# Transformer block of 2048 tokens: attention output of blocks 2 to 14 turned by transposing transfers, values of eight heads in one stretch, another count for row tilings

## The chip, the cores and the metric

The program runs on one core of a Trainium2 chip. The metric is the time of one execution in microseconds of the device, median of several runs; lower is better. TensorE (PE) does the matrix products, VectorE (DVE) and ScalarE (ACT) the work element by element, GpSimd (POOL) the selects of the mask, SyncE (SP) issues most transfers. Each engine takes its instructions in the order in which they were written into the program.

## The reference

One transformer block, all in float32: S = 2048 tokens of D = 640, 32 heads of 20 with a causal window of 256 keys, and a gated feed-forward part of 1536.

```python
def _layernorm(x, axis=-1, eps=1e-5):
    m = jnp.mean(x, axis=axis, keepdims=True)
    v = jnp.var(x, axis=axis, keepdims=True)
    return (x - m) / jnp.sqrt(v + eps)

def _A_ref(x, wqkv, wo):
    ...
    q, k, v = qkv[0], qkv[1], qkv[2]
    scores = jnp.einsum("bhqd,bhkd->bhqk", q, k) * (Dh ** -0.5)
    idx = jnp.arange(S)
    mask = (idx[:, None] - idx[None, :] >= 0) & (idx[:, None] - idx[None, :] < W)
    scores = jnp.where(mask[None, None], scores, -1e9)
    p = _softmax(scores, axis=-1)
    o = jnp.einsum("bhqk,bhkd->bhqd", p, v)
    return (lambda x, *d: x.transpose(*d))(o, 0, 2, 1, 3).reshape(B, S, D) @ wo

def _B_ref(x, w_gate, w_up, w_down):
    return (_gelu(x @ w_gate) * (x @ w_up)) @ w_down

x = A_x
h = x + _A_ref(_layernorm(x, axis=-1), A_wqkv, A_wo)
h2 = h + _B_ref(_layernorm(h, axis=-1), B_w_gate, B_w_up, B_w_down)
```

## The kernel before

**Staging.** The tokens are cut into 16 blocks of 128. For each block x is loaded and normalised, split into a high and a low float16 part (`xh`, `xl`) and turned, so that the features lie on the partitions. Q and K are made for two blocks at a time, V for one. Every dense product is the sum of three float16 products (high by high, high by low, low by high), which stand in the profile as matmuls on `mm` with weights such as `w0h` and `w0l`. The feed-forward part comes last, after the attention of all blocks; its first pieces begin while the last blocks' attention runs.

**Attention of a block.** For each pair of heads the scores are made twice. First with queries on the partitions (`maxima`, line 833): 60 rows of the array, two heads side by side on its two halves, into `ra` or `rb`, a tile of two PSUM banks each. VectorE adds the band of the mask and reduces each head's 320 scores to the row's maximum `mxs` in one instruction (`max_out`, line 905), which writes the masked scores as bf16 into `junk`. Then with keys on the partitions (`scores`, line 950), with two more rows that carry the maxima, again into `ra` or `rb`. ScalarE takes the exponential into `pt` (`score_out`, line 988), and GpSimd sets to zero what lies outside the window: three `affine_select` for four heads at once where a block has three key blocks. `pt` is a ring of three tiles, each with four heads. The values (`value_lane`, line 1015) are float32 products of 128 rows by 21 columns, four heads on the four column groups of the array, 24 records for four heads, into `pv`. After 16 heads `pv` is copied to `oT`, four transposes and a division bring it back to rows as `o32` (`normalise`, line 1041).

**The attention output.** `o_transpose` (line 1062) turns the 128x640 of `o32` on TensorE with the identity: four chunks of 128 into `tp`, then the fifth. ScalarE casts `tp` to `oh`, VectorE subtracts to `ol`. Both are the weights that stay in the array for the output projection (`wo_block`, line 1080). There is one buffer of `tp`.

**x by transfers.** Blocks of x from the fifth on (`x_lane`, line 673) are turned another way, by `turned` (line 505): ScalarE casts x to float16 in the first half of a buffer `xp`, VectorE writes the rest into the second half, and SyncE issues two transposing transfers, `xh<-xp` and `xl<-xp`. `xp` has one buffer, and a counter (`opened["xparts"]`) lets only one block into it at a time, until the second transfer has been issued.

**What sets the order.** Nothing is scheduled by hand. The builder keeps a clock for each engine (`Clock`, line 54) and gives every instruction a modelled duration (`Engine.cost`, line 214). Each piece of work is a generator that yields the engine it needs and the time at which its data are there by that model. The loop at the end of `block_kernel` picks, again and again, the first of its lanes that can start: results that come out of PSUM, transposes, the row lane (`maxima` and `scores`), the value lane, and the dense lane. So a changed duration, or a changed wait, moves instructions on all engines. For TensorE the model adds 0.095 us where the form changes between full, row (64 rows or less) and column (32 columns or less), and counts a matmul beside the previous one, on another part of the array, almost at nothing:

```python
switch, k.mode = SWITCH * (k.mode != mode), mode
...
beside, k.half = mode != "full" and at > k.half and not switch, at
if beside:
    return 0.004
return switch + k.warmth(max(n * passes / 2400, 0.027), rows) + 0.0027
```

All instructions carry line 199, where the wrapper calls the real engine; the names of the tiles tell them apart.

Of the kernel before, what the change touches and what calls it, by code (L numbers as in the profile page):

```python
# [11 lines left out]
F32 = mybir.dt.float32  # L12
F16 = mybir.dt.float16
BF16 = mybir.dt.bfloat16
# [8 lines left out]
P = 128  # L23
# [166 lines left out]
class Engine:  # L190
# [23 lines left out]
    def cost(self, op, out, ins):  # L214
# [39 lines left out]
def block_kernel(ctx: ExitStack, tc: tile.TileContext, x, wqkv, wo, wg, wu, wd, out):  # L254
# [87 lines left out]
    ones = const.tile([P, P], F32, name="ones")  # L342
    nc.vector.memset(ones, 1.0)
# [251 lines left out]
    mask = wp.tile([P, 2 * P], F32, name="mask")  # L595
# [3 lines left out]
    band = wp.tile([P, 5 * HB], F32, name="band")  # L599
# [11 lines left out]
    RV, RK = 5, 6  # L611
# [101 lines left out]
    def load_x(j):  # L713
        if 0 < j < NR:
            t = at("pt", [P, 4, 3, P], F32, 3).rearrange("p a b c -> p (a b c)")
# [98 lines left out]
    def pairs(j):  # L814

        return 2 if j < 2 else 1
# [42 lines left out]
    def row_need():  # L859
# [45 lines left out]
    def max_out(j, pr, par, ps, at_):  # L905
        b = B[j]
        n = len(window(j))
        for k in range(pairs(j)):
# [3 lines left out]
            junk = at("junk", [P, 5 * HB], BF16, 1)  # L912
            nc.vector.tensor_tensor_reduce(junk[:, :w], head,
# [36 lines left out]
    def scores(at_):  # L950
        j, pr = scoreq.popleft()
        b = B[j]
        u = pr // 2
        if pr % 2 == 0:
            b.pt[u] = at("pt", [P, 4, 3, P], F32, 3)
            pos["units"] += 1
# [21 lines left out]
        tasks.append(score_out(j, pr, t, b.pt[u], at_))  # L978
# [9 lines left out]
    def score_out(j, pr, t, pt, at_):  # L988
        b = B[j]
        u = pr // 2  # L990
        n = len(window(j))
        m = pairs(j)
        yield on("scalar", t)
        w = min(n * P, 5 * HB)
        for k in range(m):
            h = 2 * (pr % 2 + k)
            nc.scalar.activation(pt[:, h:h + 2].rearrange("p h a b -> p h (a b)")[:, :, :w],
                                 t[:, :, k * n * P:k * n * P + w], AF.Exp, scale=esc)
# [5 lines left out]
        if n == 3:  # L1004
            half = pt.rearrange("p h a (b c) -> p h (a b) c", b=2)
            for a, (i, o) in enumerate(((0, 0), (3, 5))):
                nc.gpsimd.affine_select(half[:, :, o], half[:, :, i], pattern=[[0, 4], [-1, HB]],
                                        compare_op=ALU.is_ge, fill=0.0, base=-1 - HB * a,
                                        channel_multiplier=1)
        diag = part(pt, n, n - 1).rearrange("p h a b -> p h (a b)")  # L1010
        nc.gpsimd.affine_select(diag, diag, pattern=[[0, 4], [1, P]],
                                compare_op=ALU.is_ge, fill=0.0, base=0, channel_multiplier=-1)
        valq.append((j, u))

    def value_lane():

        while True:
            yield pe(when=lambda: valq and B[valq[0][0]].v == 2 and pos["ones"])
            j, u = valq.popleft()
            b = B[j]  # L1020
            pt = b.pt.pop(u)
# [3 lines left out]
            yield pe(pt, pv[:, u % 4, :])  # L1025
            for k, i in enumerate(order):
                for c in range(4):
                    nc.tensor.matmul(pv[32 * c:32 * c + DH + 1, u % 4, :].rearrange(
                                         "p (a b) -> p a b", b=HB),
                                     vring[ks[i] % RV][:, 4 * u + c, :], part(pt, n, i)[:, c],  # L1030
                                     start=(k == 0), stop=(k == n - 1))
            pos["values"] += 1
# [664 lines left out]
```

## Time and profile before

| | |
|---|---|
| median of three runs | 1022.17 us (1020.41 to 1023.81) |
| the profiled execution | 1023.17 us |
| its span, from first to last instruction | 1021.3 us |
| granted TensorE clock, mean | 1.000 |
| transposes of the attention output on TensorE, `tp<-ident,o` | 80 records, 15.0 us busy, 286 ns each |
| row maxima of 320 scores on VectorE | 448, 219.1 us busy, 489 ns each |
| selects of the mask on GpSimd, `pt<-pt` | 352, 175.3 us busy, 513 ns each |
| values, `pv<-pt,v`, four heads | 24 records, 0.85 us |

The page's first part gives the busy time of each engine and its share of the span, with the number of instructions. A busy TensorE is not the same as TensorE at its peak, since matmuls overlap and their ends are modelled. The groups give, for one kind of instruction by the names of its tiles, its count, its busy time, the mean of one in ns, and the idle time of the engine just before it with what ended it. In a timeline a row is: start in us, duration, engine, line, operation, what it writes and reads, shapes, and in brackets the idle time ahead of it and its releaser. For TensorE the shape 60*64 means 60 rows by 64 columns of the array.

### The profile page before, as it was taken

To read this page: it belongs to the slowest core of one execution; us is meant where nothing else is said; L and a number is where in the kernel's file an instruction comes from. 1 tells how busy PE (TensorE), PEld (TensorE's weight loads), DVE (VectorE), ACT (ScalarE), POOL (GpSimd) and SP (SyncE) were. 2 spreads that over 40 slices of the span, in tenths; PEclk is the share of its full clock that TensorE was granted. 3 is DMA by queue.
4 is the path that set the end of the run, shared out by engine and by line. 5 is a ranking of instruction groups with operands and counts; after the bars stand their busy time and mean duration, and the time that the engine had idled before them with its cause. 6 is when DMAs were issued, how large, how long until landed. Compare 5 with 4: busy or idle time off the path is not lost.

```text
span 1021.3 us, 30777 instructions
## 1 busy us (share of the span) xinstructions
PE 999.8 (98%) x12921; PEld 695.8 (68%) x12921; DVE 754.8 (74%) x2221; ACT 437.0 (43%) x706; POOL 298.0 (29%) x489
## 2 busy tenths in 40 slices
PE   8999999999999999999999999999999999999998
PEld 7875666676666676776655564567777777777776
DVE  6888998986787787474788788798996975544553
ACT  6514654656555564654558543522222222221220
POOL 7102223443343342342436321255313310000000
PEclk9999999999999999999999999999999999999999
DMA  8657667361551524225033433223553532222211
GB/s 306 137 116 175 184 145 168 81 163 55 91 122 44 114 57 118 42 61 127 3 131 106 92 117 103 78 104 127 161 177 90 161 138 78 78 96 86 78 53 52
DMA packets 105835, 112.67 MB, mean 110 GB/s; under 512 B 38369, under 2 KB 79585, under 8 KB 105697
## 3 DMA queue, kind: packets, MB, share of 16 engines
q1 hardware_dynamic: 93600, 99.97, 35.9%
q10 hardware_dynamic: 12096, 10.75, 3.4%
q8 instruction: 101, 1.65, 0.7%
q14 instruction: 38, 0.30, 0.1%
HBM read 73.73 MB, written 28.84 MB: 100 GB/s over the span
## 4 chain that ended last, share of the span: by engine, by line
PE 82%; DVE 8%; DMA 4%; ACT 2%; issue 2%; SPq 1%; POOL 0%; ACTq 0%; DVEq 0%
PE mm L199 41%; PE pv L199 12%; PE ra L199 11%; PE rb L199 10%; PE tp L199 7%; DVE junk L199 2%; DVE am L199 1%; DVE ht L199 1%; DMA v<-in_wqkv_dram 1%; DMA gu<-in_wqkv_dram 1%; SPq L199 1%; DMA qT<-mT 1%; DVE m L199 1%; ACT pt L199 1%; DMA h_dram<-ht 1%
## 5 line engine op out<-in xcount | busy, mean ns | idle before, releaser
L199 POOL TENSOR_SCALAR_AFFINE_SELECT pt<-pt 128x512 f32<-128x512 f32 x352 | 175.3, 513 | 278.2 <-ACT pt L199 262.6
L199 DVE CUSTOM_DVE_ANT_0 junk<-rb,band 128x320 bf16<-128x320 f32 x230 | 112.5, 489 | 41.3 <-PE rb L199 35.9
L199 DVE CUSTOM_DVE_ANT_0 junk<-ra,band 128x320 bf16<-128x320 f32 x218 | 106.6, 489 | 43.8 <-PE ra L199 38.3
L199 ACT ACTIVATE pt<-ra,esc 128x640 f32<-128x640 f32 (+2 forms) x131 | 99.6, 767 | 66.2 <-PE ra L199 53.3
L199 ACT ACTIVATE pt<-rb,esc 128x640 f32<-128x640 f32 (+2 forms) x125 | 94.9, 766 | 77.2 <-PE rb L199 56.5
L199 PE MATMUL pv<-pt,v 128*21 128x128 f32 x2880 | 104.1, 275 | 1.1 <-ACT oT L199 1.1
L199 PEld LDWEIGHTS <-ah 128*128 128x128 f16 x768 | 75.0, 98 | 29.5 <-issue 2.1
L199 ACT ACTIVATE gel<-gel,ffk 128x512 f32<-128x512 f32 x36 | 26.0, 721 | 138.0 <-DVE gel L199 138.0
L199 PEld LDWEIGHTS pv<-pt,v 128*21 128x21 f32 x2880 | 68.6, 100 | 11.9 <-issue 2.1
L199 PEld LDWEIGHTS <-ws 128*128 128x128 f16 x720 | 70.3, 98 | 8.3
L199 PEld LDWEIGHTS <-kT 62*64 62x64 f16 x2880 | 61.9, 107 | 13.9 <-issue 10.1
L199 PEld LDWEIGHTS <-qT 60*64 60x64 f16 x1280 | 29.8, 104 | 60.3 <-issue 51.3
L199 PEld LDWEIGHTS <-gu 128*128 128x128 f16 x440 | 42.1, 98 | 36.1 <-issue 2.5
L199 DVE SCALAR_TENSOR_TENSOR ht<-mm,ffk,ht 128x320 f32<-128x320 f32 x96 | 52.1, 545 | 10.9 <-PE mm L199 9.0
L199 ACT CAST ah<-gel 128x512 f16<-128x512 f32 x48 | 29.6, 617 | 64.4 <-DVE gel L199 64.2
L199 PE MATMUL mm<-xh,w1h 128*128 128x256 f16 x200 | 54.7, 274 | 1.3 <-DVE qks L199 1.3
L199 PE MATMUL mm<-xl,w1h 128*128 128x256 f16 x200 | 54.7, 273 | 0.0
L199 PE MATMUL mm<-xh,w1l 128*128 128x256 f16 x200 | 54.7, 273 | 0.0
L199 PE MATMUL mm<-w3l,oh 128*128 128x320 f16 x160 | 48.1, 301 | 0.1
L199 PE MATMUL mm<-w2h,xh 128*128 128x320 f16 x160 | 48.1, 300 | 0.0
L199 PE MATMUL mm<-w2h,xl 128*128 128x320 f16 x160 | 48.1, 301 | 0.0
L199 PE MATMUL mm<-w3h,ol 128*128 128x320 f16 x160 | 48.1, 300 | 0.0
(299 smaller groups left out, 2521.3 us busy)
## 6 DMA issues: line engine op xcount, KB each, us to landing
ws<-wsums SPq DMA_DIRECT2D x24, 640.0 KB
qk<-qks ACTq DMA_DIRECT2D x32, 256.0 KB
qT<-qk SPq DMA_DIRECT2D x48, 160.0 KB
kT<-qk SPq DMA_DIRECT2D x48, 160.0 KB
wsums<-ws SPq DMA_DIRECT2D x12, 640.0 KB
ht<-in_x_dram SPq DMA_DIRECT2D x16, 320.0 KB
h_dram<-ht SPq DMA_DIRECT2D x16, 320.0 KB
ht<-h_dram SPq DMA_DIRECT2D x16, 320.0 KB
```

Of the source, the lines that this page charges most:

```text
L199: r = real(*args, **kw)
```

## The change

- *Count of row tilings.* In the builder's clock a matmul beside the last one, on another part of the array, counts 0.0005 us in place of 0.004.
- *Row maxima.* `tensor_tensor_reduce` writes its masked scores back to the PSUM that it reads; `junk` is gone. `mask` and `band` become bf16. The constant `ones` is dropped.
- *Exponentials.* The ring `pt` has seven tiles of two heads in place of three of four. GpSimd's selects go over two heads at a time, so there are twice as many of half the size. A part of the ring is free again when the values of its group of four are made.
- *Values.* The value lane waits for two groups of four heads and writes both in one stretch, 48 records instead of 24.
- *Attention output.* For blocks 2 to 14 `o_transpose` goes through `turned`, as x does: a cast on ScalarE into `xp`, a subtraction on VectorE, and two transposing transfers into `oh` and `ol` on SyncE. It shares `xp` and its counter with x. Blocks 0, 1 and 15 stay on TensorE.

```diff
@@ Engine.cost
             if beside:
-                return 0.004
+                return 0.0005
...
-    mask = wp.tile([P, 2 * P], F32, name="mask")
+    mask = wp.tile([P, 2 * P], BF16, name="mask")
...
-    band = wp.tile([P, 5 * HB], F32, name="band")
+    band = wp.tile([P, 5 * HB], BF16, name="band")
...
-    RV, RK = 5, 6
+    RV, RK, RP = 5, 6, 7
...
@@ row_need
-        free = 3 - (pos["units"] - pos["values"])
+        free = RP - (pos["parts"] - 2 * pos["values"])
         for j, pr in list(scoreq)[:2]:
             b = B[j]
-            free -= pr % 2 == 0
+            free -= pairs(j)
...
@@ max_out
-            junk = at("junk", [P, 5 * HB], BF16, 1)
-            nc.vector.tensor_tensor_reduce(junk[:, :w], head,
+            nc.vector.tensor_tensor_reduce(head, head,
                                            band if n == 3 else mask[:, (2 - n) * P:], 1.0,
                                            -3.0e38, ALU.add, ALU.max,
...
@@ scores
-        if pr % 2 == 0:
-            b.pt[u] = at("pt", [P, 4, 3, P], F32, 3)
-            pos["units"] += 1
+        for k in range(pairs(j)):
+            b.pt[pr + k] = at("pt", [P, 2, 3, P], F32, RP)
+        pos["parts"] += pairs(j)
...
@@ score_out
-        pos[j, u] += 2 * m
-        if pos[j, u] < 4:
-            return
-        yield on("gpsimd", pt[:, :, 0, :])
...
+        for k in range(pr, pr + pairs(j)):
+            pt = b.pt[k]
+            yield on("gpsimd", pt[:, :, 0, :])
+            if n == 3:
...
+            diag = part(pt, n, n - 1).rearrange("p h a b -> p h (a b)")
+            nc.gpsimd.affine_select(diag, diag, pattern=[[0, 2], [1, P]],
+                                    compare_op=ALU.is_ge, fill=0.0, base=0, channel_multiplier=-1)
+            pos[j, "u", k // 2] += 1
+            if pos[j, "u", k // 2] == 2:
+                valq.append((j, k // 2))
...
@@ value_lane
-            yield pe(when=lambda: valq and B[valq[0][0]].v == 2 and pos["ones"])
-            j, u = valq.popleft()
+            yield pe(when=lambda: len(valq) > 1 and B[valq[0][0]].v == 2 and pos["ones"])
+            j, u = valq[1]
...
-            yield pe(pt, pv[:, u % 4, :])
...
+            yield pe(*(b.pt[k] for k in range(2 * u - 2, 2 * u + 2)),
+                     pv[:, u % 4 - 1:u % 4 + 1, :])
+            for u in (u - 1, u):
...
@@ o_transpose
+        if 2 <= j < 15:
+            def dst():
+                b.oh, b.ol = at("oh", [P, KC, P], F16), at("ol", [P, KC, P], F16)
+                return b.oh, b.ol
+
+            yield on("scalar", src, when=lambda: not opened["xparts"] and B[j - 2].wrote)
+            yield from turned(src, None, None, dst, None, at("xp", [P, D], F32, 1))
+            b.normal = True
+            woq.append(j)
+            return
```

`turned`, which the change calls and does not touch:

```python
key = "xparts" if dst else "parts"
yield on("scalar", src, when=lambda: not opened[key] and (not when or when()))
opened[key] += 1
two = (two if dst else lnbuf[2]).bitcast(F16)
hi, lo = two[:, :D], two[:, D:]
nc.scalar.copy(hi, src)
yield on("vector", hi)
nc.vector.tensor_tensor(lo, src, hi, op=ALU.subtract)
if dst:
    to = dst()
for o, i in zip(to, (hi, lo)):
    yield ("sync",), need(i, eng="sync")
    nc.sync.dma_start_transpose(o, i)
opened[key] -= 1
```

Where the instructions stand. On TensorE, before, in the middle of the attention: one group's values (`pv`, of the exponentials `pt`) between a row tiling (`rb`) and the transposes of the attention output (`tp<-ident,o32`).

```order
L199 LDWEIGHTS kT_124
L199 MATMUL rb_7857<-qT_5631,kT_124 64x64
L199 MATMUL pv_125<-pt_7729,v3_122 21x128 x4
L199 MATMUL pv_125<-pt_7729,v2_121 21x128 x4
L199 MATMUL pv_125<-pt_7729,v4_123 21x128 x4
L199 MATMUL tp_7890<-ident_78,o32_7496 128x128 x4
L199 LDWEIGHTS w0h_144
L199 MATMUL mm_7753<-xl_5821,w0h_144 128x256
```

On TensorE of the changed kernel, the same kind of place (of the second group, `pt_6855` and `pt_6895`, the first key block is shown):

```order
L199 MATMUL mm_6945<-w2h_158,xl_2530 128x320
L199 MATMUL pv_123<-pt_6770,v1_118 21x128 x2
L199 MATMUL pv_123<-pt_6824,v1_118 21x128 x2
L199 MATMUL pv_123<-pt_6770,v0_117 21x128 x2
L199 MATMUL pv_123<-pt_6824,v0_117 21x128 x2
L199 MATMUL pv_123<-pt_6770,v2_119 21x128 x2
L199 MATMUL pv_123<-pt_6824,v2_119 21x128 x2
L199 MATMUL pv_123<-pt_6855,v1_118 21x128 x2
L199 MATMUL pv_123<-pt_6895,v1_118 21x128 x2
```

The values of two groups now follow one another, each group from two tiles of `pt`, and no transposes of `o32` come behind.

On VectorE, before, within one block's row maxima (`mxs`; the reads of the accumulator between the reductions are left out):

```order
L199 ISA junk_7066,mxs_5633<-ra_7046,band_105 128x320
L199 ISA junk_7108,mxs_5633<-rb_7078,band_105 128x320
L199 SCALAR_TENSOR_TENSOR ht_5735<-mm_7038,hsc_128,ht_5735 128x320
L199 ISA junk_7155,mxs_5633<-ra_7128,band_105 128x320
L199 RECIPROCAL rec_7154<-tp_7149 128x16
L199 TENSOR_TENSOR o32_6806<-tp_7149,rec_7154 128x320
L199 ISA junk_7191,mxs_5633<-rb_7170,band_105 128x320
```

On VectorE of the changed kernel, again within one block's maxima:

```order
L199 ISA ra_7300,mxs_5534<-ra_7300,band_103 128x320
L199 BN_STATS lstx_7352<-xt_5989 128x6
L199 SCALAR_TENSOR_TENSOR ht_6383<-mm_7251,hsc_126,ht_6383 128x320
L199 BN_AGGR lmvx_7382<-lstx_7352 128x2
L199 ISA ra_7359,mxs_5534<-ra_7359,band_103 128x320
L199 RECIPROCAL rec_7395<-tp_7390 128x16
L199 TENSOR_TENSOR o32_7389<-tp_7390,rec_7395 128x320
L199 ISA ra_7400,mxs_5534<-ra_7400,band_103 128x320
```

Each reduction stands there twice, once for each head of the pair, and is shown once. Before, the maxima take `ra` and `rb` in turn; now they go into `ra` three times, one fill after the other, with the scores in `rb`.

On SyncE of the changed kernel, with the transfers of the attention output between a store of the residual stream (`h_dram`) and loads of x and of the queries:

```order
L199 DMA h_dram_72<-ht_4756 128x640
L199 DMA ht_6383<-in_x_dram 128x640
L199 DMA_TRANSPOSE oh_6414<-xp_6376 128x5x128
L199 DMA_TRANSPOSE ol_6415<-xp_6376 128x5x128
L199 DMA h_dram_72<-ht_5403 128x640
L199 DMA qT_6998<-qk50_5637 20x16x256 x3
```

The two transposing transfers are new in this queue; before, the loads and stores follow one another there.

More of the change, by code (lines that the diff above doesn't have):

```diff
@@ L341, in block_kernel @@
     nc.vector.memset(mhalf, -0.5)
-    ones = const.tile([P, P], F32, name="ones")
-    nc.vector.memset(ones, 1.0)
     NS = 16
@@ L986, in part, with score_out @@
         return (half[:, :, 0:6:5], half[:, :, 1:3], half[:, :, 3:5])[i]
-    def score_out(j, pr, t, pt, at_):
+    def score_out(j, pr, t, at_):
         b = B[j]
-        u = pr // 2
         n = len(window(j))
-        m = pairs(j)
+        w = min(n * P, 5 * HB)
         yield on("scalar", t)
[L994 to L997, printed above, removed]
+        for k in range(pairs(j)):
+            nc.scalar.activation(b.pt[pr + k].rearrange("p h a b -> p h (a b)")[:, :, :w],
@@ L1024, in value_lane @@
             order = [1, 0, 2] if n == 3 else list(range(n))
-            yield pe(pt, pv[:, u % 4, :])
[L1026 to L1032, printed above, removed]
+            yield pe(*(b.pt[k] for k in range(2 * u - 2, 2 * u + 2)),
+                     pv[:, u % 4 - 1:u % 4 + 1, :])
+            for u in (u - 1, u):
+                valq.popleft()
+                pt = [b.pt.pop(k) for k in (2 * u, 2 * u + 1)]
+                for k, i in enumerate(order):
+                    for c in range(4):
+                        nc.tensor.matmul(pv[32 * c:32 * c + DH + 1, u % 4, :].rearrange(
+                                             "p (a b) -> p a b", b=HB),
+                                         vring[ks[i] % RV][:, 4 * u + c, :],
+                                         part(pt[c // 2], n, i)[:, c % 2],
+                                         start=(k == 0), stop=(k == n - 1))
+                pos["values"] += 1
             if u % 4 == 3:
```

21 lines of the change are left out of this document (7 added, 14 removed).

## Prediction

> **What bounds the kernel now.** I read the page's busy times first, then its chain of waits, then the table of stretches of 50 us.
>
> ```profile
> span 1021.3 us, 30777 instructions
> ...
> PE 999.8 (98%) x12921; PEld 695.8 (68%) x12921; DVE 754.8 (74%) x2221; ACT 437.0 (43%) x706; POOL 298.0 (29%) x489
> ...
> PE 82%; DVE 8%; DMA 4%; ACT 2%; issue 2%; SPq 1%; POOL 0%; ACTq 0%; DVEq 0%
> ...
> core 0: us, PE busy (x) PEld busy (x) DVE busy (x) ACT busy (x) POOL busy (x), PEclk, DMA share, GB/s
> ...
> 100.00:150.00 50.00, 48.47 (x801) 33.26 (x794) 46.69 (x158) 29.71 (x52) 14.22 (x26) 1.00 0.64 155
> 150.00:200.00 50.00, 47.68 (x796) 33.20 (x794) 44.60 (x160) 28.73 (x48) 17.14 (x34) 1.00 0.54 142
> ...
> 400.00:450.00 50.00, 49.78 (x1012) 34.62 (x1010) 30.00 (x112) 25.07 (x40) 17.05 (x37) 1.00 0.23 61
> ```
>
> TensorE works without a real break and its clock is granted in full: time goes only where PE gets less to do, and comes back where PE has to wait. VectorE is the neighbour to watch: from 100 to 200 us it is busy 91.3 of 100 us, while at 400 to 450 us it has 20 us of 50 free. The profiled execution took 1023.17 us, 1.9 more than its span and 1.0 more than the median of 1022.17; I sum against 1023.2 and take off 1.0 at the end.
>
> **Term 1: changes of tiling.** TensorE's own line of time shows what leaving one form of matmul for another costs (start in us, duration, what is written and read, rows*columns of the array, shapes).
>
> ```profile
> 301.86 0.27 PE L199 MATMUL mm<-xh,w0l 128*128 128x256 f16 x1
> 302.06 0.33 PE L199 MATMUL rb<-kT,qT 60*64 60x320 f16 x4
> 302.22 0.31 PE L199 MATMUL ra<-qT,kT 62*64 62x128 f16 x12
> 302.46 0.85 PE L199 MATMUL pv<-pt,v 128*21 128x128 f32 x24
> ...
> 303.37 0.27 PE L199 MATMUL mm<-xl,w1h 128*128 128x256 f16 x1
> 303.48 0.27 PE L199 MATMUL mm<-xh,w1l 128*128 128x256 f16 x1
> ```
>
> Equal dense matmuls of 256 columns start 0.11 us apart (303.37 to 303.48). Where a row tiling (60*64, 62*64) follows the same dense matmul, the step is 0.20 (301.86 to 302.06). A change of form thus costs 0.09; from one row group to another (302.06 to 302.22) there is none. Counted over the whole order, dense, row and column (128*21) matmuls change places 657 times before and 569 times after: stretches of the 24 value records fall from 128 to 64, of 48 records each. 88 changes by 0.09 are **7.9 us** less PE work.
>
> **Term 2: transposes of the attention output.** The same line of time where the five chunks of one block's output are turned, four together and the fifth later:
>
> ```profile
> 306.59 0.66 PE L199 MATMUL tp<-ident,o 128*128 128x128 f32 x4
> 307.18 0.33 PE L199 MATMUL ra<-kT,qT 60*64 60x320 f16 x4
> ...
> 309.96 0.33 PE L199 MATMUL tp<-ident,o 128*128 128x128 f32 x1
> 310.13 0.27 PE L199 MATMUL mm<-xh,w1l 128*128 128x256 f16 x1
> ```
>
> Four take 0.59 with a change behind them, so 0.50; the fifth 0.17. 13 blocks by 0.67 are **8.7 us** less. PE work falls by 16.6 us in all; nothing is added to it.
>
> **Term 3: refills of the maxima's banks.** The new order sends the row maxima into the bank that held the last maxima 129 times of 239, before 28 times. What such a refill needs:
>
> ```profile
> 463.11 0.34 PE L199 MATMUL rb<-kT,qT 60*64 60x128 f16 x8
> ...
> 463.50 0.49 DVE L199 CUSTOM_DVE_ANT_0 junk<-rb,band 128x320 bf16<-128x320 f32 x1 [0.60 <-PE rb L199]
> ...
> 464.03 0.49 DVE L199 CUSTOM_DVE_ANT_0 junk<-rb,band 128x320 bf16<-128x320 f32 x1
> ...
> 464.72 0.34 PE L199 MATMUL rb<-kT,qT 60*64 60x128 f16 x8
> ...
> 98.47 0.49 DVE L199 CUSTOM_DVE_ANT_0 junk<-rb,band 128x320 bf16<-128x320 f32 x1
> ...
> 99.03 0.11 PEld L199 LDWEIGHTS <-qT 60*64 60x64 f16 x4 [1.02 <-DVE mxs L199]
> ```
>
> VectorE starts 0.39 after the fill, two reductions take 0.53 and 0.49, and a waiting PE goes on 0.07 after them (98.96 to 99.03): a floor of 1.48 us from fill to fill, or 1.61 if the 0.20 of 464.72 were needed. Laid out along PE's order with the steps above, the shortest refill before is 1.54 us; after, 38 are under 1.47 and together lack 1.6 us, and 68 are under 1.61 and lack 9.3. I take **+3 us**, nearer to the floor that a wait shows. This holds if a reduction costs the same when it writes PSUM in place as when it writes bf16 to SBUF, which no row has. The nearest are the fills:
>
> ```profile
> L199 DVE MEMSET pv<- 128x512 f32 x1 | 0.5, 485 | 0.1
> ...
> L199 DVE MEMSET ident<- 128x128 f32 x1 | 0.2, 165 | 0.9 <-PEq L1684 0.9
> ...
> L199 DVE MEMSET mhalf<- 128x1 f32 x1 | 0.1, 59 | 0.0
> ```
>
> 59 and 165 ns in SBUF lie on a line of 0.835 ns per element that gives 486 at 512; PSUM took 485, so writing there was not dearer, and I take nothing. The bounds: a reduction without its write could hardly save over 0.07, about 2 us over the tight refills; one that reads and writes a bank in turns would take another 320 elements, 0.33 us, on 448 reductions.
>
> **Term 4: where VectorE is full.** From 80 to 250 us lies a third of the saving, some 5.8 us. VectorE's work per block stays what it was there, with 8.7 us free in the 100 shown, much of it waits for fills. I give back half, **+3 us** (0 to 5.8). Past 250 us the free time covers it.
>
> **Term 5: what the transfers bring.**
>
> ```profile
> L199 DVE RECIPROCAL rec<-tp 128x16 f32<-128x16 f32 x32 | 8.1, 253 | 2.6 <-PE tp L199 2.5
> ...
> L199 DVE TENSOR_TENSOR o<-tp,rec 128x320 f32<-128x320 f32 x32 | 15.6, 488 | 0.6
> ...
> L199 ACT CAST oh<-tp 128x512 f16<-128x512 f32 x16 | 9.3, 582 | 8.1 <-PE tp L199 8.1
> ...
> L199 ACT CAST xp<-xt 128x640 f16<-128x640 f32 x12 | 8.7, 721 | 8.2 <-DMA xl<-xp 7.0 <-DVE xt L199 1.2
> ...
> L199 DVE TENSOR_TENSOR ol<-tp,oh 128x512 f16<-128x512 f32 x16 | 11.0, 686 | 3.3 <-ACT oh L199 3.3
> ...
> L199 DVE TENSOR_TENSOR xp<-xt,xp 128x640 f16<-128x640 f32 x12 | 10.4, 864 | 0.6 <-ACT xp L199 0.6
> ...
> L199 SPq DMA_TRANSPOSE xh<-xp x12: 1201/1339/2580, 46.7 to 371.1; - x12
> ...
> 198.94 0.71 ACT L199 CAST xp<-xt 128x640 f16<-128x640 f32 x1
> ...
> 199.68 2.40 SPq L199 DMA_TRANSPOSE xh<-xp  x1
> ...
> 207.21 0.72 ACT L199 CAST xp<-xt 128x640 f16<-128x640 f32 x1
> ...
> 275.44 0.71 ACT L199 CAST xp<-xt 128x640 f16<-128x640 f32 x1
> ...
> 284.82 0.73 ACT L199 CAST xp<-xt 128x640 f16<-128x640 f32 x1 [1.57 <-DMA xl<-xp]
> ```
>
> A block's cast and subtraction cost 0.72 and 0.86 in place of 0.58 and 0.69 for four fifths and one more of each: even on both engines. SyncE gets 26 issues of about 1.34, 35 us, among loads that have that room. But all share one buffer, xp, held from its cast until the second transfer has landed: at most 8.3 us in one case (198.94 to 207.21, no wait shown), 9.4 in another. In the new order two casts of x follow three or four ScalarE rows behind one of o. They will wait, with exponentials queued behind them whose banks PE wants: **+2 us** (0 to 6). The output projection's matmuls stand 7.4 to 20.7 us of PE work behind the last transpose of oT, seven of thirteen under 10: **+1 us** (0 to 22, the slower rival below).
>
> The Trainium skill, "VectorE: DVE Perf Modes", section "The three transpose paths", speaks against the change: it gives 1309 ns for a 128x128 tile by transposing transfer and 390 by TensorE. Its ten tiles a block would be 13.1 us; the trace had ten done within 7.5 (199.68 to 207.21), so the measurement decides.
>
> **Term 6: selects.**
>
> ```profile
> L199 POOL TENSOR_SCALAR_AFFINE_SELECT pt<-pt 128x256 f32<-128x256 f32 x224 | 89.9, 425 | 246.6 <-ACT pt L199 246.4
> ...
> L199 POOL TENSOR_SCALAR_AFFINE_SELECT pt<-pt 128x512 f32<-128x512 f32 x128 | 85.3, 667 | 31.7 <-ACT pt L199 16.3 <-issue 2.7 <-PE ra L199 2.5
> ```
>
> They become 448 of 128 elements (by the line through 425 and 667, 0.30) and 256 of 256: 245 us for 175. GpSimd has 14 to 17 us of work in 50, so there is room for 70 more. After the last exponential of a group 1.03 us remain (0.30 twice, 0.425) where 1.52 did (0.425 twice, 0.667), and three parts may run ahead of the stretch that waits: **nothing**. Without that cover values would come late by some tenths in 64 stretches.
>
> **Sum.** 16.6 less, 3 + 3 + 2 + 1 more: 7.6 less, 1015.6 against the profiled execution, **1015 us** against the median.
>
> **Rivals.**
> - *All of it pays.* No refill waits beyond the floor, VectorE finds its room, the casts wait on nobody: 1022.2 - 16.6 + 1.6, or 1007. For it: idle VectorE past 250 us. Against: the two full stretches. Chance 0.13 (up to 1011).
> - *VectorE takes it back.* PE stands at the same bank again and again: 9.3 us at the longer floor, 5.8 in the full stretch, 2 for the casts come to 17: no change, 1020 to 1025. For it: 68 refills shorter than any comfortable one before. The same result if the counting that shapes the order moves work without shortening it; the 88 changes speak against that. Chance 0.23.
> - *Projections wait on transfers.* PE takes its queue in order, so each block's first matmul on oh holds everything behind it. Its chain is 0.3 to 0.5 of transposes (o's four took 0.50), 0.25 and 0.49 on VectorE, some 0.4 of hand-overs (an estimate from the 0.39 after a fill), then 8.3 to 9.4 or more until both transfers land. At 10.8 us the seven short blocks lack 13 us, at 12.0 they lack 22: 1027 to 1036. It turns the result once cast to landing takes over some 9 us as a rule, as it did at 275.44, behind K and Q loads. Against: 8.3 was only an upper bound. Chance 0.12.
> - *Reductions in place are dear.* If the engine reads and writes a bank in turns, 448 reductions take up to 0.33 more, 148 us on an engine with 266 to spare in all but under 9 in the 100 us shown; what lands in the full stretch and in the 129 same-bank refills is paid for: 129 by 0.66 is 85 us at most, 1022 - 17 + 20 to 85, so 1025 to 1090. Against: the fills of PSUM and SBUF above, on one line. Chance 0.03.
> - *Transfers nearly twice as slow.* If a block's ten tiles took 13 us instead of the 7.5 seen, the chain from the last transpose of oT would be 15.7, eleven of thirteen blocks would wait, and together they lack 51 us: near 1066. Against it stands the 7.5 of the trace itself. Chance 0.02. The Trainium skill's 1309 ns, cited above, would lead here.
>
> **How the numbers follow.** Forecast 0.47 (1011 to 1019), full gain 0.13, no change 0.23, slower 0.17. A measurement of this kernel tells apart about 0.3%, 3 us: faster 0.60, same 0.23, slower 0.17. The range runs from 1005, the whole saving kept, to 1028, where the slower rival begins.
>
> **What would show it.** PE busy down by about 16, with the tp<-ident,o group at 15 records in place of 80 and the weight loads' idle time before qT and kT smaller. Term 3: PE's weight loads wait on mxs oftener than now, and reductions of 489 ns still. Term 4: VectorE over 95% busy in 100 to 200 us. Term 5: casts of xp that wait on ol or xl, and matmuls on oh that wait on a DMA. I am wrong if the reductions change their duration, or if waits on oh exceed 5 us together.

## The result, and the profile after

The changed kernel takes **1030.47 us** (1029.11 to 1031.95, four runs) against 1022.08 of the kernel before in the same comparison: ratio 1.0091, 95% interval 1.0075 to 1.0107. It is slower by 0.9%, where 1015 was forecast and 1028 was the upper end of the range.

The page of the changed kernel, its span, busy times and chain:

```profile
span 1027.4 us, 31093 instructions
...
PE 994.9 (97%) x12845; PEld 695.4 (68%) x12845; DVE 769.3 (75%) x2207; ACT 432.6 (42%) x693; POOL 365.6 (36%) x841
...
PE 69%; DVE 17%; issue 4%; DMA 4%; POOL 2%; ACT 2%; SPq 0%; DVEq 0%; ACTq 0%; POOLq 0%
```

VectorE's share of the chain that ended last went from 8% to 17%, and TensorE's fell from 82% to 69%: TensorE now waits where it used to work. From the starts of the matmuls in both traces, the time from each one's start to the next, summed by kind, shows both sides. "Waits" are the parts of these times that exceed the usual step between two such matmuls by more than 0.06 us.

| us | before | after |
|---|---|---|
| transposes in float32 | 32.2 | 21.9 |
| values | 97.0 | 90.8 |
| maxima and scores | 110.9 | 119.9 |
| dense and the rest | 775.0 | 788.8 |
| sum | 1015.1 | 1021.4 |
| waits within it | 20.7 | 44.2 |
| sum without waits | 994.4 | 977.2 |

TensorE's work fell by 17.2 us (forecast: 16.6). Its waits rose by 23.5 (forecast: 9 for all terms together). The list of waits of the weight loads names whom they are for. Before:

```profile
PEld L199 <- DVE mxs L199: 5.4, 20, 1.0
```

After:

```profile
PEld L199 <- DVE mxs L199: 42.5, 120, 1.0
PEld pv L199 <- POOL pt L199: 3.7, 9, 0.7
PEld L199 <- DMA ol<-xp: 0.8, 1, 0.8
```

Columns of a list of waits are the sum in us, the times, the longest. Some 0.2 of each wait is the ordinary gap at a change of form; a weight load of the trace before has 0.21 with nothing awaited:

```profile
463.11 0.29 PEld L199 LDWEIGHTS <-qT 60*64 60x64 f16 x16 [0.21 <-issue]
```

So of the 42.5 us some 17 are real waits for the maxima, and of the 5.4 before some 1. The transfers of the attention output, on which the slower rival rested, are waited for once here.

The groups of VectorE show what the reductions became. Before:

```profile
L199 DVE DVE_READ_ACCUMULATOR2_ANT mxs<- 128x1 f32 x512 | 42.3, 83 | 0.0
```

After:

```profile
L199 DVE CUSTOM_DVE_ANT_0 ra<-ra,band 128x320 f32<-128x320 f32 x270 | 134.4, 498 | 47.9 <-PE ra L199 33.1 <-PE rb L199 10.0
...
L199 DVE DVE_READ_ACCUMULATOR2_ANT mxs<- 128x1 f32 x512 | 72.3, 141 | 0.0
...
L199 PE MATMUL tp<-ident,o 128*128 128x128 f32 x15 | 2.9, 289 | 0.4 <-DVE ol L199 0.2
```

The reduction itself shows 498 ns for 489. But the read of the accumulator behind it, which ends the instruction, takes 141 for 83 on the mean of the 512. A pair of reductions in the changed kernel:

```profile
299.56 0.49 DVE L199 CUSTOM_DVE_ANT_0 rb<-rb,band 128x320 f32<-128x320 f32 x1
299.97 0.14 DVE L199 DVE_READ_ACCUMULATOR2_ANT mxs<- 128x1 f32 x1
300.15 0.50 DVE L199 CUSTOM_DVE_ANT_0 rb<-rb,band 128x320 f32<-128x320 f32 x1
300.56 0.14 DVE L199 DVE_READ_ACCUMULATOR2_ANT mxs<- 128x1 f32 x1
```

From one reduction to the next it is 0.59 us, where it was 0.53 (463.50 to 464.03). An instruction of another kind behind a reduction starts 0.42 after it in both kernels (the median of each trace), so VectorE's busy time rose by 14.5 us in all, not by 0.06 for each of the 512. A bank pays twice, in the second reduction's later start and in its later end. Two fills of `rb` in the changed kernel, the second waiting for the maxima of the first:

```profile
214.53 0.33 PE L199 MATMUL rb<-kT,qT 60*64 60x320 f16 x4
...
216.11 0.11 PEld L199 LDWEIGHTS <-qT 60*64 60x64 f16 x4 [0.31 <-DVE mxs L199]
```

They stand 1.58 us apart, where the floor of the prediction was 1.48. The stretch in which the waits rose most, before:

```profile
50.00:100.00 50.00, 47.92 (x575) 32.82 (x572) 41.38 (x187) 15.23 (x34) 4.27 (x7) 1.00 0.63 144
```

After, with the two in which VectorE had been full:

```profile
50.00:100.00 50.00, 42.37 (x514) 29.54 (x512) 41.44 (x174) 15.11 (x34) 8.48 (x18) 0.97 0.73 158
100.00:150.00 50.00, 48.11 (x684) 32.38 (x685) 48.49 (x165) 26.90 (x47) 12.06 (x30) 1.00 0.62 158
150.00:200.00 50.00, 48.32 (x910) 34.50 (x913) 42.41 (x149) 29.50 (x46) 26.42 (x79) 1.00 0.49 136
```

VectorE is at 97% from 100 to 150 us (93% before) and at 85% from 150 to 200 us (89% before). From 50 to 100 us TensorE's waits alone grew from 2.8 to 10.7 us, and its granted clock is 0.97 there, for 1.00 before. Closer by, that is one stretch at half the clock:

```profile
84.50:87.90 3.40, 1.26 (x21) 0.74 (x19) 3.23 (x14) 0.58 (x3) 0.77 (x2) 1.00 0.76 241
87.90:91.30 3.40, 3.40 (x32) 2.12 (x31) 2.38 (x10) 1.62 (x4) 0.77 (x2) 0.50 0.74 156
```

TensorE worked 1.26 of 3.40 us, and in the next 3.4 us it was granted half its clock, which is worth some 1.7 us (an estimate, half of 3.4). A long wait can thus cost more than itself; in one of the runs below that is most of the loss.

### The profile page after: what moved, and what is told of

It is laid out like the page before. It is cut to its first block, busy times and chain, and to the rows that moved or that the text cites. A ratio compares the mean times of both kernels' runs of the same rounds, so it can differ in the third digit from the quotient of the medians.

```text
span 1027.4 us, 31093 instructions
## 1 busy us (share of the span) xinstructions
PE 994.9 (97%) x12845; PEld 695.4 (68%) x12845; DVE 769.3 (75%) x2207; ACT 432.6 (42%) x693; POOL 365.6 (36%) x841
## 4 chain that ended last, share of the span: by engine, by line
PE 69%; DVE 17%; issue 4%; DMA 4%; POOL 2%; ACT 2%; SPq 0%; DVEq 0%; ACTq 0%; POOLq 0%
PE mm L199 33%; PE ra L199 11%; PE pv L199 10%; PE rb L199 9%; PE tp L199 5%; DVE ra L199 4%; DVE rb L199 4%; POOL pt L199 2%; DVE mxs L199 2%; DVE am L199 1%; DMA kT<-qk 1%; DMA ol<-xp 1%; DVE qks L199 1%; DMA h_dram<-ht 1%; DVE ht L199 1%
## 5 line engine op out<-in xcount | busy, mean ns | idle before, releaser
L199 POOL TENSOR_SCALAR_AFFINE_SELECT pt<-pt 128x128 f32<-128x128 f32 (+1 forms) x704 | 242.1, 362 | 233.7 <-ACT pt L199 211.9
L199 DVE CUSTOM_DVE_ANT_0 ra<-ra,band 128x320 f32<-128x320 f32 x270 | 134.4, 498 | 47.9 <-PE ra L199 33.1
L199 ACT ACTIVATE pt<-rb,esc 128x640 f32<-128x640 f32 (+2 forms) x152 | 116.9, 775 | 93.0 <-PE rb L199 73.4
L199 DVE CUSTOM_DVE_ANT_0 rb<-rb,band 128x320 f32<-128x320 f32 x178 | 88.5, 497 | 19.2 <-PE rb L199 10.4
L199 ACT ACTIVATE pt<-ra,esc 128x640 f32<-128x640 f32 (+2 forms) x104 | 77.9, 757 | 59.4 <-PE ra L199 44.3
L199 PE MATMUL pv<-pt,v 128*21 128x128 f32 x2880 | 94.0, 274 | 1.3 <-POOL pt L199 1.1
L199 DVE DVE_READ_ACCUMULATOR2_ANT mxs<- 128x1 f32 x512 | 72.3, 141 | 0.0
L199 PE MATMUL ra<-kT,qT 60*64 60x320 f16 (+4 forms) x768 | 48.6, 280 | 6.9 <-DVE mxs L199 2.9
L199 POOL TENSOR_TENSOR gelt<-gelt 128x256 f32<-128x256 f32 x18 | 15.2, 846 | 112.0 <-ACT gelt L199 111.9
L199 POOL TENSOR_TENSOR rr<-rr 128x256 f32<-128x256 f32 x18 | 14.9, 831 | 108.9 <-ACT rr L199 108.9
```

The source lines that it names most:

```text
L199: r = real(*args, **kw)
```

## The experiments

All times are medians; "before" is the kernel before, run beside each.

### The write in place, and the order

Two things changed for the reductions: where they write, and when the builder thinks they are done. Its clock gave a reduction of 320 elements 0.065 + 0.00106 x 320 = 0.404 us (`Engine.cost`). In the kernel before, the one buffer of `junk` made the next reduction wait 0.18 more in that clock (`Clock.tile` and `LAT`), 0.584 in all, near the chip's 0.53. Without `junk` the clock says 0.404 and the chip 0.59. These runs take the two apart.

**sbuf_write_same_order**: the order of the changed kernel, the write of the kernel before.

```diff
-            nc.vector.tensor_tensor_reduce(head, head,
...
+            nc.vector.real.tensor_tensor_reduce(junk[:, :w], head, add, 1.0, -3.0e38,
+                                                ALU.add, ALU.max, acc)
+            nc.issue("vector", nc.vector.cost("tensor_tensor_reduce", head, [head, add]),
+                     [head, add], [head, acc])
```

> The changed kernel with its order kept row by row, but the reductions write bf16 to SBUF as before (into the mask's tile for blocks from 2 on, into a tile of the feed-forward part that is still unused for blocks 0 and 1). Theory (the write to PSUM in place holds the end of each reduction back by the 58 ns that the accumulator reads grew by, and the refills of the same bank pay for it): reads of the accumulator at 83 ns again, waits of PE's weight loads on mxs from 42.5 us down to 10 to 20, time 1016 to 1022. Rival 1 (the order alone is at fault, the place of the write is immaterial): 1028 to 1031. Rival 2 (the transfers of the attention output are at fault: SyncE, the buffer xp, the projections): 1028 to 1031.

1024.15 us, ratio to before 1.0010 (0.9993 to 1.0028): 6 us less than the changed kernel by the medians, 8 by the ratios. The group of the accumulator's reads:

```profile
L913 DVE DVE_READ_ACCUMULATOR2_ANT mxs<- 128x1 f32 x512 | 42.2, 82 | 0.1
```

And its list of waits:

```profile
PEld L199 <- DVE mxs L913: 31.5, 107, 0.9
```

The reads are back at 82 ns, so it is the write in place that delays them. Whether by its place (PSUM) or by its type (float32 for bf16) isn't separated, since both changed together; the bf16 mask is not it, as the reads stay at 82 with it here and are 141 without it in the next run. But 107 waits on the maxima stay, with some 9 us beyond the ordinary gap for the 17, and 40.4 us of waits in all: most of the waits belong to the order. The time was 2 us above the forecast, the waits well above the 10 to 20 expected.

**inplace_in_old_order**: the reverse, the kernel before with its order kept and `junk[:, :w]` replaced by `head` as the place written.

> The kernel before with its order kept row by row, but each reduction writes back to PSUM in place. Theory: reads of the accumulator at 141 ns, some 31 us more work on VectorE, and as the old order leaves 1.54 us and more to a refill, only 1 to 6 us more: 1023 to 1028. Rivals 1 and 2: 1021 to 1023.

1023.84 us, ratio 1.0015 (0.9997 to 1.0033). The reads are at 141 ns and VectorE is busy 770.2 us for 754.8, yet hardly any of it is paid (by the interval nothing to 3 us). Where refills have room, the write in place is nearly free.

**inplace_alone**: the same instructions, but the order is left to the clock (the edit is that of the change: `tensor_tensor_reduce(head, head, ...)`, no `junk`, bf16 masks).

> The kernel before with only the reductions in place and the bf16 mask; the order is free to follow the builder's clock, which no longer waits for the one buffer of junk. Theory: many refills of the same bank that are too short for a reduction in place (by the order they lack 15 us if a refill needs 1.61 us, 3.7 us if 1.48): 1028 to 1036. Rival 1 (order alone, a refill needs 1.48): 1021 to 1024. Rival 2 (transfers): 1020 to 1023.

**1051.86 us**, ratio 1.0299 (1.0257 to 1.0340). This one edit costs 29 us, more than the whole change does. Its waits:

```profile
PEld L199 <- DVE mxs L199: 47.1, 137, 1.0
PE ra L199 <- DVE mxs L199: 4.8, 10, 0.8
```

The second line is mostly the same waits as the first, seen from the matmul behind the weight load. TensorE's work without waits is 994.5, as before (994.4); its waits are 49.3 for 20.7. Its granted clock was 0.993 for 1.000, which by itself is some 7 us of the 1050 (an estimate). The forecast had the direction and not the size: the lacking time was laid out along TensorE's order alone; the clock was not in it, nor what queues behind a late reduction on VectorE, whose share was not measured.

**inplace_order_sbuf_write**: that order row by row, with the write to SBUF.

> The order of inplace_alone row by row, but the reductions write bf16 to SBUF. Theory A: most of the 29 us stays, 1038 to 1048 (the write gave 6 us in the order of the changed kernel). Theory B: 1022 to 1027.

1041.86 us, ratio 1.0181 (1.0150 to 1.0211). So some 19 of the 29 us are the order's and 10 those of the write in it: theory A.

**inplace_clock_charged**: `inplace_alone`, with the 0.18 us that the one buffer of `junk` had added in the clock as a wait now added to each reduction's length.

```diff
+            m += 170 * (op == "tensor_tensor_reduce")
             return 0.065 + 0.00106 * m + 0.06 * (op == "scalar_tensor_tensor" and len(ins) == 3)
```

> The kernel of inplace_alone (before, reductions in place), but the builder's clock charges 0.18 us more for each reduction, as much as the wait for the one buffer of junk had added to it. Theory A (the price of inplace_alone is the order, made by a clock that thinks a reduction takes 0.40 us where the chip needs 0.59): near the kernel before again, 1023 to 1030, waits on mxs below 20 us. Theory B (the write in place itself, 141 instead of 83 ns at the end of each): stays above 1045.

1027.65 us, ratio 1.0062 (1.0038 to 1.0086). One number in the builder's clock takes back 24 of the 29 us, and the granted clock of the profiled execution is 1.000 again:

```profile
PEld L199 <- DVE mxs L199: 5.8, 19, 1.3
```

### The clock in the changed kernel

**changed_clock_charged**: the same line in the changed kernel.

> The changed kernel with 0.18 us more charged by the clock for each reduction; nothing else. Theory A in its simple form (a clock that is right about the reduction makes a good order): 1006 to 1014. Theory C (an order is as good as the room it leaves, and this one leaves short refills elsewhere: laid out by the steps of TensorE its maxima lack 28 us at 1.61 and its scores as much again, mostly from 400 to 450 us): 1040 to 1060.

1059.69 us, ratio 1.0368 (1.0322 to 1.0414), in the range of theory C. Fewer waits on the maxima, but others, and stretches of a lower clock:

```profile
PEld L199 <- DVE mxs L199: 15.1, 26, 1.4
PE ra L199 <- ACT pt L199: 11.4, 13, 3.2
PE rb L199 <- ACT pt L199: 9.5, 12, 1.6
```

```profile
450.00:500.00 50.00, 41.13 (x875) 29.13 (x871) 31.60 (x111) 23.33 (x34) 23.74 (x75) 0.80 0.29 54
```

The granted clock of this execution is 0.975 on the mean, for 0.998 in the changed kernel. Of its 1059 us that is some 26 (an estimate, 0.025 of the span), for 2: most of the 32 us between the two profiled executions. So the price is in large part the half clock that follows long waits, and theory C, which speaks of short refills alone, isn't shown by its time. A builder's clock that was right about this one instruction did not make a good order here; why the new order waits so long on the exponentials was not found.

**clock_half_charged**: 0.085 us more in place of 0.18, so 0.489 in the builder's clock, and the old count of row tilings.

```diff
+            m += 80 * (op == "tensor_tensor_reduce")
...
-                return 0.0005
+                return 0.004
```

> The changed kernel with 0.085 us more charged for each reduction, and row tilings beside one another counted 0.004 as before. Laid out, its refills lack 2.3 us (maxima at 1.61) and 5.1 (scores), and TensorE's work is as little as in the changed kernel. Theory C: 1006 to 1015. If the waits come from something else that all forms of the change share (the transfers, the paired values, the selects): 1020 to 1030.

1017.75 us, ratio 0.9938 (0.9909 to 0.9967): 13 us less than the changed kernel with the same work on every engine, though 3 above the forecast's end. The two edits were not run apart in this kernel; in the kernel before, the count alone is the next run but one.

**half_charged_sbuf_write**: that order with the write to SBUF.

> The order of clock_half_charged row by row, but the reductions write bf16 to SBUF. If the price of the write in place is paid only where a refill is tight (29 waits on mxs and 10 us here, 120 and 43 us in the changed kernel, where it came to 6 us): 0 to 4 us less than clock_half_charged, 1013 to 1018. If every reduction pays (512 by 0.06 us on VectorE): 8 us less or more.

1015.62 us, ratio 0.9931 (0.9908 to 0.9953). 2 us for the write, which the intervals don't separate from none; not 8.

**beside_alone**: the kernel before with only 0.0005 for 0.004.

> The kernel before with only the other count for row tilings beside one another. It adds and removes no instruction; only the order follows. By the order laid out TensorE does 1 us less and its refills lack 1 us more: 1020 to 1025 if the layout tells what an order is worth. Outside that: any new order costs or gains several us by itself, whatever part of the change made it.

1022.68 us, ratio 0.9979 (0.9962 to 0.9996): nothing to speak of.

### The transfers

**o_on_tensor**: the changed kernel with all blocks' outputs turned on TensorE.

```diff
-        if 2 <= j < 15:
+        if False:
```

> The changed kernel with the attention output of all blocks turned on TensorE again, everything else as changed. Theory: 8 us more on TensorE, and the waits on mxs stay above 35 us in all: 1034 to 1039. Rival 2 (the transfers are at fault): the waits fall with them, 1018 to 1026.

1029.18 us, ratio 1.0067 (1.0042 to 1.0092), which the intervals don't separate from the changed kernel. Both expected times missed, though the weight loads' waits on the maxima stayed at 35.7, as the theory had it. TensorE's transposes take 31.0 us for 21.9, and its waits 34.4 for 44.2. With the transfers, and in the order that comes with them, TensorE has 9 us less work and 10 us more waits.

**half_charged_o_on_tensor**: the same edit in `clock_half_charged`.

> clock_half_charged with the attention output of all blocks turned on TensorE again. TensorE's transposes 8.7 us more; by the order laid out, its refills lack 5.8 us less. If the transfers gain on TensorE but bring an order with shorter refills: 1017 to 1024. If they gain what TensorE saves: 1025 to 1028. If they cost more than they save (SyncE, xp, contention): below 1015.

1014.59 us, ratio 0.9926 (0.9896 to 0.9955): no slower with TensorE doing the transposes, and waits of 24.0 for 34.2. The medians differ by 3 us and the ratios by 0.12%; the intervals overlap.

**transfers_alone**: the kernel before with only the new `o_transpose`.

> The kernel before with only the attention output of blocks 2 to 14 by transfers. TensorE's work falls by 9 us; the order laid out lacks 9 us more for the maxima and 6 us more for the scores. If the order is the price: 1021 to 1030. If the transfers keep what they save: 1013 to 1017. If the projections wait on them as the slower rival had it: waits of TensorE on the transfers of 5 us or more.

**1037.79 us**, ratio 1.0148 (1.0109 to 1.0187), 8 us above the upper end expected. Its waits:

```profile
PE mm L199 <- DMA oh<-xp: 2.3, 2, 2.1
...
PEld L199 <- DVE mxs L199: 13.3, 27, 1.6
PEld L199 <- DMA oh<-xp: 2.7, 2, 2.4
```

Here the projections wait for the transfers: 2.7 us on `oh` by the weight loads and 0.9 on `ol`, 3.6 in all, less than the 5 that the expectation named. (The line of the matmuls on `mm` shows the same two waits on `oh` once more.) The other waits, some 15 of the 18 us added, have several owners, the maxima first.

**transfers_own_buffer**: `transfers_alone`, with a buffer `xo` and a counter `oparts` for the output, and bf16 masks to make the room.

> transfers_alone, with a buffer and a counter of their own for the attention output, apart from x's (bf16 mask and band make the room). If transfers_alone loses its 15 us to the shared buffer (casts that wait for landings, exponentials queued behind them): 1015 to 1024. If it loses them to its order or to the transfers themselves: 1030 to 1040.

1028.16 us, ratio 1.0045 (1.0029 to 1.0062): between the two expectations. 10 us less than with the shared buffer, though its order differs too, and still slower than before.

What sharing looks like is seen in the changed kernel's own line of time, with rows of ScalarE, SyncE and TensorE (in brackets the wait and its releaser):

```profile
211.36 0.72 ACT L199 CAST xp<-o 128x640 f16<-128x640 f32 x1 [2.06 <-DVE o L199]
...
214.18 1.22 SPq L199 DMA_TRANSPOSE ol<-xp  x1
...
216.11 0.33 PE L199 MATMUL rb<-kT,qT 60*64 60x320 f16 x4
...
216.85 0.72 ACT L199 CAST xp<-xt 128x640 f16<-128x640 f32 x1 [2.44 <-DMA ol<-xp]
217.48 0.79 ACT L199 ACTIVATE pt<-ra,esc 128x640 f32<-128x640 f32 x1
...
218.32 0.34 PE L199 MATMUL ra<-qT,kT 62*64 62x128 f16 x12 [1.88 <-ACT pt L199]
```

The output's second transfer is issued at 214.18 and lands by 216.85. The cast of x stands at the head of ScalarE's queue until then, the exponential behind it starts at 217.48, and TensorE waits 1.88 us for the bank which that empties. The clock let the cast of x go this early because x's buffer had been asked for before the output's transfers were issued.

**changed_xp_in_clock**: the changed kernel, where such a cast is held until the clock has the last transfer out of `xp` landed.

```diff
+        yield ("scalar",), lambda: max(free(), nc.quiet(used[-1]) + nc.LAT if dst and used else 0.0)
```

> The changed kernel, but a cast into xp is not put into ScalarE's queue before the clock has the last transfers out of xp landed (the clock took x's buffer as free from an earlier time). The waits of ScalarE on ol<-xp, 4.5 us in two, go; the order laid out is otherwise like that of the changed kernel, with 2 us more lacking. If those casts cost TensorE what they seem to (2.05 us at 216): 1026 to 1030. If not: 1030 to 1035.

1031.24 us, ratio 1.0066 (1.0043 to 1.0090): no gain over the changed kernel. ScalarE's waits on `ol<-xp` are gone, but TensorE's waits in the new order are 49.2 for 44.2, so what those casts cost could not be told from what the new order costs.

### The values, and the parts together

**half_charged_values_single**: `clock_half_charged` with four heads to a stretch again.

```diff
-            yield pe(when=lambda: len(valq) > 1 and B[valq[0][0]].v == 2 and pos["ones"])
+            yield pe(when=lambda: valq and B[valq[0][0]].v == 2 and pos["ones"])
...
```

> clock_half_charged with the values of four heads in a stretch of their own again, from the ring of seven parts. Some 4 us more on TensorE by the order laid out, refills as before. If pairing is worth its changes of form: 1019 to 1025. If the wait for a second group costs more than that: 1010 to 1016.

1032.69 us, ratio 1.0099 (1.0067 to 1.0131): 15 us slower, 8 beyond the range. The values' steps are 104.7 us for 91.1, waits between them among that, and the waits in all are 41.1 for 34.2. The granted clock is 0.990 for 0.997, by itself some 7 us (an estimate from the two spans). Pairing pays here, by more than its changes of form, but half of that may be the clock and the rest is also another order.

**half_charged_o_on_tensor_sbuf**: paired values, the split ring, the old count of row tilings, half the charge, the transposes on TensorE, the write to SBUF.

> half_charged_o_on_tensor row by row, but the reductions write bf16 to SBUF: the parts of the change that paid, without the two that did not. Its refills lack nothing at 1.61 us, so the cheaper write should give little: 1011 to 1015; 1006 to 1010 if VectorE's 30 us less count in full somewhere.

**1011.13 us**, ratio 0.9860 (0.9837 to 0.9883). It beats both kernels: by 1.4% the kernel before, 12.7 us in this comparison, and by 19 us the changed one. Run again as **parts_that_pay_again**:

> The same kernel as half_charged_o_on_tensor_sbuf, run beside the next one so that the two can be compared: 1010 to 1014.

1011.42 us, ratio 0.9889 (0.9870 to 0.9909), 11.8 us under the kernel before.

**three_transposes_left_out**: this order kept row by row on every engine, 39 transposes fewer.

```diff
...
+            if less and c > c0:
+                nc.issue("tensor", nc.tensor.cost("transpose", o, [i, ident]), [i, ident], [o])
+            else:
+                nc.tensor.transpose(o, i, ident)
...
```

> The same kernel with its order kept row by row, but of the attention output of blocks 2 to 14 three of the five transposes on TensorE are left out (chunks 1 to 3 of each block repeat chunk 0, so the output projection gets other numbers); ScalarE and VectorE do what they did. 39 transposes of 0.125 us are 4.9 us less for TensorE. If TensorE's work counts in full where the order stays: 4 to 6 us less than parts_that_pay_again. If waits elsewhere take it back even then: 0 to 2 us less.

1013.10 us, ratio 0.9899 (0.9878 to 0.9921), against 0.9889 for its base. Nothing was gained. The group of transposes, in the base:

```profile
L199 PE MATMUL tp<-ident,o 128*128 128x128 f32 x80 | 14.5, 279 | 0.4 <-DVE o L199 0.4
```

With the three left out:

```profile
L199 PE MATMUL tp<-ident,o 128*128 128x128 f32 x41 | 10.8, 299 | 1.4 <-DVE ol L538 1.0 <-DVE o L199 0.4
```

TensorE's steps for transposes fell by 3.8 us (30.2 to 26.4), and its waits rose from 21.9 to 29.3: some before the second part of an output's transposes, on `ol`; some on weight sums and on transfers of the queries, which the edit doesn't touch. Two executions of the base itself differ by some 3 us in their waits, so not all of the rise is the edit's. These 39 transposes, taken off TensorE, weren't worth their time, even with the order unchanged.

## Why the prediction was wrong

- **Terms 1 and 2, TensorE's work.** Right in size: 17.2 us less for a forecast of 16.6, with 10.3 off the transposes and 6.2 off the values. The account they stand in, that time goes where TensorE has less to do and comes back where it waits, adds up too: 1015.1 - 17.2 + 23.5 = 1021.4. But less work and more waits came together. The transfers' share gave no time that could be measured in either pair of runs (o_on_tensor, half_charged_o_on_tensor), and three_transposes_left_out gained nothing with nothing else moved. A busy share of 98% did not tell this.
- **Term 3, refills, is the step that failed.** It was put at 3 us. The weight loads' waits on the maxima, less the ordinary gap, rose from some 1 us to some 17, which is 13 more than forecast, of a miss of 15. It failed in two halves. "I take nothing" for the write in place: the floor from fill to fill is 1.58 us (214.53 to 216.11) and not 1.48, since both reductions of a pair end later; worth 6 us by the medians (8 by the ratios) in the changed order and 1 in the old. And the time lacking along TensorE's order as the price of the refills: with the write back in SBUF, so with the forecast's own premise, some 9 us of waits on the maxima stay, where the layout lacked 1.6 at a floor of 1.47 and the term took 3. The count of 129 same-bank refills was the right sign, priced too low. The prediction saw that the refills had become short and didn't ask why: the builder's clock had lost 0.18 us for each reduction.
- **Term 4, VectorE full.** In the full stretches its work was indeed the same, 90.9 us from 100 to 200 us for 91.3, and TensorE's waits of 100 to 250 us rose from 7.0 to 11.4, 4.4 for the 3 forecast. Wrong was "Past 250 us the free time covers it": 27.1 of the 42.5 us of waits on the maxima lie there, 79 of the 120, where before there were 2.4 in 10. Idle time of VectorE on the mean doesn't help a refill that is short. The sign "over 95% busy in 100 to 200 us" held for the first half alone.
- **Term 5, the transfers.** The waits named were seen at about their size: two casts on `ol<-xp`, 4.5 us on ScalarE, and 0.8 us of TensorE on the transfers. A block's ten tiles with cast and subtraction took 5.5 us (211.36 to 216.85). The Trainium skill, "VectorE: DVE Perf Modes", section "The three transpose paths", gives 1309 ns for one 128x128 tile, which would be 13.1 us for the ten (an estimate); this trace doesn't agree either, and the transfers' speed was not what cost the time.
- **Term 6, the selects.** 242 us for a forecast of 245, and the weight loads of the values wait 3.7 us on them in nine places, where nothing was forecast.
- **The granted clock.** It was taken as full and stood in no term. In the changed kernel that missed some 2 us (0.998 of 1027).
- **The rivals.** Two slower rivals' ranges held the time, but neither by its mechanism. "Projections wait on transfers" (1027 to 1036): TensorE waits 0.8 us on the transfers in the changed kernel. "Reductions in place are dear" (1025 to 1090): they are dearer, which the prediction named as a sign of being wrong, but by 0.06 us where the rival had 0.33. Nearest by mechanism is "VectorE takes it back", beyond its size: 23.5 us of waits for the 17 it allowed.

What stays open: why the transfers bring waits of their own with them. In transfers_alone 3.6 of 18 us are the projections', and a buffer apart takes 10 us back, but each such edit also made a new order, and the part of each was not separated. That the lost 0.18 us makes the short refills is shown in the kernel before (inplace_alone, inplace_clock_charged). In the changed kernel the full charge made things worse, and the half charge came together with the old count, so there it is argued and not shown.

## What to carry to other kernels

When a planner's clock sets the order, an edit that removes a buffer also removes the wait that the clock charged for it: compare the clock's time for the instruction with the chip's before and after, here 0.584 against 0.53 and then 0.404 against 0.59, since in the kernel before that one line moved the time by 24 us. Then run it: in the changed kernel the same line cost 29 us, and half of it gained 13. Look at the granted clock of each run before its waits are explained. Price a saving on the busiest engine by a run that takes the work out with the order kept, since a share of 98% doesn't say that it pays. And try the parts of a change one by one: here one cost 29 us alone, one 15, and the rest, with the builder's clock set for it, made the kernel some 12 us faster than before.

## What the runs showed of the hardware

A reduction with an accumulator that writes its elements back to PSUM in float32 shows almost the same duration as one that writes bf16 to SBUF (498 and 489 ns), but the read of its accumulator ends later (it takes 141 ns for 83), for 128 columns as for 320. The next reduction starts 0.59 us after it in place of 0.53; another instruction starts 0.42 after it in both. With the order kept, VectorE was busy 770.2 us for 754.8 by that alone.

The traces of all runs have 39 stretches of 3.4 to 10.2 us, the ends of the program left out, in which TensorE was granted half its clock. In the 3.4 us ahead of each, TensorE had been busy 55% of the time or less, and the trace of the kernel before, which has no such stretch, shows a mean of 1.000. The ten executions of inplace_clock_charged, one kernel with one order, run from 1025.2 us at a mean clock of 1.000 to 1033.9 at 0.994.
